# Weights converted in wider pieces, a smaller first group of chunks, and more seven-product pairs, in one kernel of retention and two MLPs

## The chip, the cores and the metric

The kernel runs on one core of one Trainium2 chip. The metric is the device time of one execution in microseconds, as the median of several runs. Inputs and weights lie in the chip's memory when it starts.

## The reference, cut to what matters

```python
# attention: B=4, H=8, S=576, D=64, with a decay mask in place of a softmax
scores = (q @ k.T) / sqrt(D)
ret = scores * where(i >= j, gamma[h] ** (i - j), 0.0)
x = (ret @ v)                       # laid out as 2304 tokens x 512
# first MLP, 512 -> 2048 -> 512
h = maximum(x @ moe_w_in, 0.0)
y = (h * h) @ moe_w_out
# second MLP, 512 -> 1536 -> 512
out = ((y @ moe2_w_a) * (y @ moe2_w_b)) @ moe2_w_out
```

The weights arrive as 64-bit floats, as pairs of 32-bit words. The rest is float32.

## The kernel before, in words

**Precision.** A float32 operand of a matmul is split into two parts of a shorter type (float32r): a high part, copied by ScalarE, and a low part, the difference, by VectorE. Each product of 128 x 128 weights with a block of tokens is three matmuls: high by high, low by high, high by low.

**Weights.** `w_float` (L347) turns 128 x 512 weights from 64-bit to 32-bit floats: a 512 KB load into a raw buffer (`wraw`, later `raw`), two ScalarE instructions that read the high words (L373) and the low words (L399), and four on VectorE: clamp (L377), shift and mask (L384), sign (L392), and the addition of the rounded low words (L403). The result lies in `wf` or `wl`.

**First group of chunks.** The hidden units come in chunks of 128: 16 in the first MLP, 12 in the second. The chunks in `FIRST` (0 to 5) of the first MLP are taken while attention runs. `load_first` (L528) converts and splits their up and down weights, which stay in the slots `w0` to `w11`. `mlps` walks five blocks of tokens (four of 512, one of 256): for each chunk `up` (12 matmuls), squares, and `down` (12 matmuls). The sums of a block leave through `evac_y` to memory (`y1`). Attention's steps are woven in: for each microsecond of MLP matmuls, `RATE` says how much of attention comes (L1380).

**The other chunks** (`CHUNKS[1]`: 6 to 15, `CHUNKS[2]`: 0 to 11) are run in `rest` (L939) in three passes of 768 tokens, first MLP then second. `x_prep` makes seven combinations of the pass's input, as of a 2 x 2 block matrix, each split (`xo`; the seventh in `xb`). A unit is a pair of chunks in the first MLP, one chunk (its a and its b weights) in the second. Its up-projection is done as seven products in place of eight (`group`, L1114), six matmuls of 384 columns each. The combinations of weights are made once by `keep_pair` (L479) and stored in memory (`kept`); for each unit `piece` (L1019) loads its four pieces (512, 512, 512, 256 columns) into `w` slots and splits them. The second MLP's first piece is stored split (`parts`, `PARTS`) in pass 0 and loaded whole in the later ones.

**Down-projections** of these chunks are either plain (`plain`, 24 matmuls a chunk) or, where `SEVENS` names a run of chunks, seven products over pairs (`sevens`, L1253, 42 matmuls a pair; combinations of the weights by `keep_outs`, L501). Their weights pass through five `w` slots (`out_piece`, L1087). Sums are added into `xt` by `put` (L1208).

**Order.** All steps are put into a `Plan`, each with its engines, a modelled cost and what it reads and writes. `Plan.order` (L108) fixes one order per engine by the latest time at which each step is due; all loads and stores go out from SyncE's queue in that order. `enter` (L898) gives back attention's buffers once nothing uses them, and takes the later ones (`xo`, `raw`, `wl`, `tmp`). Conversions of later weights are steps like any others; `AHEAD` pairs of them are put ahead of `enter`.

## Time and profile before

| | us |
|---|---|
| median of 3 runs | 853.67 (851.36 to 857.92) |
| the profiled execution | 855.08 |
| its span, first to last instruction | 853.4 |
| TensorE busy in it | 835.2 (98%) |
| VectorE busy | 732.1 (86%) |
| ScalarE busy | 581.4 (68%) |

In the profile PE is TensorE's matmuls, PEld its weight loads, DVE VectorE, ACT ScalarE, SP SyncE; L234 is line 234 of the kernel, which for matmuls, copies and differences is the line of a helper. Records of neighbouring instructions of one engine overlap a little: the start of the next comes before the recorded end of the last, so what one costs its engine is read from start to start.

### The profile page before, as it was taken

What the parts mean: (1) busy time and instruction counts of PE and PEld (TensorE: products, weight loads), DVE (VectorE), ACT (ScalarE), POOL (GpSimd) and SP (SyncE); (2) the same over time, 40 slices, a digit from 0 to 9 for tenths busy, and PEclk for the clock granted to TensorE, in tenths of its full rate; (3) what the DMA queues carried; (4) which work ended last, traced back from release to release, by engine and by line L of the source; (5) the groups of instructions that cost most, each with busy time, mean ns of one, the idle gap of its engine ahead of it and who ended that gap; (6) DMA issues with size and microseconds to landing.
All of it is one profiled execution on the core that took longest, in us unless ns stands there. A gap on an engine that the chain in (4) does not pass through costs nothing.

```text
span 853.4 us, 17622 instructions
## 1 busy us (share of the span) xinstructions
PE 835.2 (98%) x6540; PEld 802.4 (94%) x6540; DVE 732.1 (86%) x1444; ACT 581.4 (68%) x1209; POOL 0.7 (0%) x6
## 2 busy tenths in 40 slices
PE   6799999999999999999999999999999999999998
PEld 6688888889999999999999999999999999999997
DVE  6999773878799998999999979989786789878785
ACT  5787663767888877878796565676556576556560
POOL 0000000000000000000000000000000000000000
PEclk9999999999999999999999999999999999999999
DMA  8966861379877667757847898755564545655432
GB/s 321 330 205 201 287 221 45 113 248 295 284 239 243 205 208 238 249 188 241 294 154 234 276 287 296 227 163 170 172 180 142 152 149 173 189 173 161 139 88 81
DMA packets 89734, 176.15 MB, mean 206 GB/s; under 512 B 9904, under 2 KB 34864, under 8 KB 89648
## 3 DMA queue, kind: packets, MB, share of 16 engines
q1 hardware_dynamic: 89504, 175.02, 64.2%
q8 instruction: 51, 0.84, 0.4%
q14 instruction: 35, 0.29, 0.1%
q10 hardware_dynamic: 144, 0.01, 0.0%
HBM read 134.75 MB, written 40.24 MB: 205 GB/s over the span
## 4 chain that ended last, share of the span: by engine, by line
PE 90%; DMA 4%; DVE 3%; ACT 2%; issue 1%; ACTq 0%
PE bank L234 90%; DMA w<-kept 2%; DMA raw<-w 1%; DVE w L243 1%; DMA vt<-vtab 0%; DVE wf L392 0%; DVE sc L731 0%; ACT w L240 0%; DVE xt L246 0%; DVE xt L698 0%; ACT bank L240 0%; DVE wf L403 0%; DVE pt L713 0%; ACT wf L373 0%; ACT sa L738 0%
## 5 line engine op out<-in xcount | busy, mean ns | idle before, releaser
L234 PE MATMUL bank<-xo,w 128*128 128x384 f32 x1838 | 389.5, 335 | 1.5 <-ACT bank L240 1.4
L234 PEld LDWEIGHTS bank<-xo,w 128*128 128x128 f32 x1838 | 324.4, 188 | 3.3 <-ACT bank L240 2.8
L234 PE MATMUL bank<-xb,w 128*128 128x384 f32 (+2 forms) x1044 | 230.1, 348 | 0.8 <-ACT r L855 0.7
L240 ACT CAST w<-w 128x512 fp32r<-128x512 f32 (+1 forms) x316 | 156.6, 518 | 81.7 <-DMA w<-kept 73.5
L234 PEld LDWEIGHTS bank<-xb,w 128*128 128x128 f32 x1044 | 183.8, 188 | 13.2 <-ACT r L855 1.1
L243 DVE TENSOR_TENSOR w<-w 128x512 fp32r<-128x512 f32 (+1 forms) x316 | 171.6, 562 | 17.9 <-ACT w L240 16.4
L234 PE MATMUL bank<-gh,w 128*128 128x384 f32 (+2 forms) x750 | 170.2, 352 | 0.0
L234 PEld LDWEIGHTS bank<-gh,w 128*128 128x128 f32 x750 | 132.3, 188 | 11.5 <-DVE gh L243 0.3
L234 PE MATMUL bank<-w,w 128*128 128x384 f32 x546 | 124.2, 335 | 0.5 <-DVE w L243 0.5
L234 PEld LDWEIGHTS bank<-w,w 128*128 128x128 f32 x546 | 97.2, 188 | 1.2 <-DVE w L243 0.9
L246 DVE TENSOR_TENSOR xt<-bank,xt 128x384 f32<-128x384 f32 x128 | 70.0, 555 | 8.7 <-PE bank L234 7.7
L240 ACT COPY bank<-bank 128x384 f32<-128x384 f32 x122 | 57.2, 469 | 18.6 <-PE bank L234 16.6
L234 PE MATMUL bank<-ghl,w 128*128 128x384 f32 x186 | 41.0, 335 | 0.0
L243 DVE TENSOR_TENSOR xo<-xt,xo 128x768 fp32r<-128x768 f32 x36 | 33.7, 955 | 1.7 <-ACT xo L240 1.7
L399 ACT ACTIVATE we<-raw 128x512 int32<-128x512 uint32 x48 | 31.8, 666 | 2.1 <-DVE wf L403 1.6
L243 DVE TENSOR_TENSOR gh<-g,gh 128x512 fp32r<-128x512 f32 (+2 forms) x40 | 24.5, 616 | 10.0 <-ACT g L858 8.7
L234 PEld LDWEIGHTS bank<-ghl,w 128*128 128x128 f32 x186 | 33.0, 188 | 0.1
L240 ACT CAST xo<-xt 128x768 fp32r<-128x768 f32 x36 | 29.1, 830 | 5.5 <-issue 5.1
L403 DVE CUSTOM_DVE_ANT_0 wf<-wf,we 128x1024 uint16<-128x1024 uint16 x45 | 30.8, 686 | 1.4 <-ACT we L399 0.9
L234 PEld LDWEIGHTS bank<-qkr 64*64 64x64 f32 x576 | 20.4, 147 | 8.1 <-DVE wf L377 3.3
L738 ACT COPY sa<-sc 128x384 f32<-128x384 f32 x16 | 14.8, 924 | 16.9 <-DVE sc L731 16.9
L234 PE MATMUL bank<-qkr 64*64 64x64 f32 x576 | 23.0, 235 | 3.3 <-DVE wf L377 2.9
(244 smaller groups left out, 971.3 us busy)
## 6 DMA issues: line engine op xcount, KB each, us to landing
w<-kept SPq DMA_DIRECT2D x167, 256.0 KB, 3.5
raw<-w SPq DMA_DIRECT2D x48, 512.0 KB, 4.6
w<-kept SPq DMA_DIRECT2D x149, 128.0 KB, 3.0
kept<-wf SPq DMA_DIRECT2D x49, 256.0 KB, 4.0
w<-parts SPq DMA_DIRECT2D x24, 512.0 KB, 3.6
kept<-wl SPq DMA_DIRECT2D x36, 256.0 KB, 4.4
wraw<-w SPq DMA_DIRECT2D x16, 512.0 KB, 6.4
vr<-vk SPq DMA_DIRECT2D x16, 448.0 KB, 4.9
```

Source lines behind the costliest of these rows:

```text
L234: T.matmul(o, l, r, start=start, stop=stop, skip_group_check=True)
L240: return lambda e: A.copy(o(), i()) if e == "ACT" else eng[e].tensor_copy(o(), i())
L243: return lambda e: eng[e].tensor_sub(o(), a(), b())
L246: return lambda e: eng[e].tensor_add(o(), a(), b())
L399: lambda e: A.activation(like(rest), lo(), AF.Copy, scale=LO_ULPS), [kraw], [ke],
L403: lambda e: V._custom_dve(ADD32_U16LIMBS, out=w().bitcast(U16), in0=w().bitcast(U16), in1=rest.bitcast(U16)),
L738: {"ACT": 540}, lambda e: A.copy(sa.rearrange("p (c d) -> p c d", d=D), by[:, :LONG - 1]), [ksc], [ksa]
```

## The change

- `FIRST` has four chunks (0 to 3), `CHUNKS[1]` twelve (4 to 15, six pairs). `RATE` is 0.5 in place of 0.35.
- `convert` takes 1024 columns (two chunks' or two kinds' weights) at a time, from one 1 MB load; only chunk 0 is converted in two pieces of 512. Two slots of 2048 columns (`wp`), one buffer for the low words (`we`, 1024), raw buffers twice as wide and half as many.
- `keep_pair` stores its combinations as two pieces, of 1024 and 768 columns, and `piece` loads and splits two in place of four. `PARTS` is empty: nothing is stored split.
- `keep_outs` is a task of its own for both MLPs; it makes combinations only for chunks that some run of `SEVENS` names. Two 256-column pieces of seven products are loaded into one 512-column slot and split by one pair of instructions.
- `SEVENS` also has the pair 10, 11 in the second MLP's pass 2, and chunks 4 to 7 in the first MLP's passes 1 and 2.
- The tasks are in one list: the first `AHEAD` (6, that is three pairs, up and down) stand ahead of `enter`. The slots `w8` to `w15` come with the later buffers. One more split tile (`ghl1`) and three more tiles (`more`) are there for intermediate results.

```diff
 
 NW = 16
 LENT = 1536
-AHEAD = 2
-FIRST = range(0, 6)
-CHUNKS = {1: range(6, 16), 2: range(0, 12)}
+AHEAD = 6
+FIRST = range(0, 4)
+CHUNKS = {1: range(4, 16), 2: range(0, 12)}
 N2 = 384
 PASSES = NT // (2 * N2)
 PIECES, OUTS = 8, 5
 RUN, LAG = {1: 2, 2: 3}, {1: 1, 2: 2.5}
-SEVENS = {(2, 0): [range(6, 12)], (2, 1): [range(0, 6), range(6, 12)], (2, 2): [range(0, 6), range(6, 10)]}
+SEVENS = {(2, 0): [range(6, 12)], (2, 1): [range(0, 6), range(6, 12)], (2, 2): [range(0, 6), range(6, 12)], (1,1):[range(4,8)],(1,2):[range(4,8)]}
 AFTER = 0.0
 SPAN = 0.8
 MORE = (2, 0, 6)
-PARTS = (0,)
-
-RATE = [0.35, 0.35, 0.35, 0.35, 0]
-
-WF, WL, WE, RAWS = 4, 4, 2, 2
+PARTS = set()
+
+RATE = [0.5, 0.5, 0.5, 0.5, 0]
+
+WP, WE, RAWS = 2, 1, 2
 SLOTS = dict(
-    g=2, r=2, gh=2, qkr=3, vr=3, tv=2, pt=2, sa=2, wraw=4, ys=4,
+    g=2, r=2, gh=2, qkr=3, vr=3, tv=2, pt=2, sa=2, wraw=2, ys=4,
 )
 
...
 
-    ring(big, "wf", [P, 512], F32, WF)
-    ring(big, "we", [P, 512], I32, WE)
+    ring(big, "wp", [P, 2048], F32, WP)
+    ring(big, "we", [P, 1024], I32, WE)
...
-    wslot = [big.tile([P, 2, 512], F32R, name=f"w{i}") for i in range(NW)]
+    ws = [big.tile([P, 2, 1024], F32R, name=f"w{i}") for i in range(len(FIRST))]
+    wslot = [w[:, j].rearrange("p (h n) -> p h n", h=2) for w in ws for j in range(2)]
     xt = big.tile([P, KT, NT], F32, name="xt")
...
 
     ring(ap, "ys", [P, 512], F32, SLOTS["ys"])
-    ring(ap, "wraw", [P, 1024], U32, SLOTS["wraw"])
+    ring(ap, "wraw", [P, 2, 1024], U32, SLOTS["wraw"])
     vt = ap.tile([P, 3 * NP], F32, name="vt")
...
+    def convert(w, kw, src, n):
+
         rest, ke = slot("we")
...
+
+        plan.add(dmac(P * 8 * n), dma(plane, source), w=[kraw], extra=exr)
         plan.add(
-            dmac(P * 4096),
-            dma(raw, lambda: like(src.bitcast(U32))), w=[kraw], extra=exr,
+            {"ACT": act(n)}, lambda e: A.activation(like(w()), hi().bitcast(F32), AF.Abs), [kraw], kw
...
-        plan.add(
-            {"DVE": dve2(512)},
+            {"DVE": dve2(n)},
...
+    def split(to, of, n, r, h, l):
+
...
+        plan.add({"ACT": act(n)}, copy(lambda: to()[0], of), r, h)
         plan.add(
             {"DVE": dve(n), "POOL": pool(n)},
-            sub(lambda: to()[:, 1, :n], of, lambda: to()[:, 0, :n]),
-            [kof, kto + (0,)], [kto + (1,)], ex,
+            sub(lambda: to()[1], of, lambda: to()[0]), r + (h if r else []), l,
         )
...
+    def fetch(to, sources, n, h, l, name, ex=()):
+
+        if name in parts:
+            plan.add(
+                dmac(P * 8 * n), dma(lambda: to()[2].bitcast(F32), lambda: parts[name]), [("parts", name)], h + l, ex
+            )
+            return
+        for cols, of, r in sources:
+            plan.add(
+                dmac(P * 4 * (cols.stop - cols.start)),
+                dma(lambda cols=cols: to()[1].bitcast(F32)[:, cols], lambda of=of: of), [r], l, ex,
+            )
+        split(lambda: to(), lambda: to()[1].bitcast(F32), n, l, h, l)
+        if name[:2] in PARTS and pass_["now"] < PASSES - 1:
+            parts[name] = dram.tile([P, 2, n], F32, name="parts" + "_".join(map(str, name)))
+            plan.add(
+                dmac(P * 8 * n), dma(lambda: parts[name], lambda: to()[2].bitcast(F32)), h + l, [("parts", name)]
+            )
...
+    def keep_pair(ph, c, src):
+
+        w, kw = slot("wp")
+        a, b = [kw + (0,)], [kw + (1,)]
+        convert(lambda: w[:, 512:1536], a + b, src, 1024)
+        combine(w, add, 0, 4, 5, b, a)
+        combine(w, sub, 1, 0, 2, [], a)
+        combine(w, sub, 4, 2, 4, a, b)
+        combine(w, sub, 6, 3, 1, a, b)
+        keep((ph, c, 0), lambda: w[:, :1024], a, 1024)
+        keep((ph, c, 1), lambda: w[:, 1024:1792], b, 768)
+
+    def keep_outs(ph, c, src):
+
+        w, kw = slot("wp")
+        a, b = [kw + (0,)], [kw + (1,)]
+        convert(lambda: w[:, 512:1536], b, src, 1024)
+        if any(c in r for k, rs in SEVENS.items() if k[0] == ph for r in rs):
+            combine(w, add, 0, 3, 5, b, a)
+            combine(w, sub, 6, 2, 3, b, a)
+            combine(w, sub, 1, 0, 2, b, a)
+            combine(w, sub, 7, 4, 1, b, a)
+            keep((ph, c, 4), lambda: w, a + b, 2048)
+        else:
+            keep((ph, c, 4), lambda: w[:, 512:1536], b, 1024)
+
+    def outs_of(ph, c, e):
+
+        c0, wide = c - (c - CHUNKS[ph][0]) % 2, kept[ph, c - (c - CHUNKS[ph][0]) % 2, 4]
+        at = {4: 512 * (c - c0), 5: -512, 6: 1024}[e] + (512 if wide.shape[1] == 2048 else 0)
+        return wide, at, ("kept", (ph, c0, 4))
+
+    tasks = []
+    for c in CHUNKS[1][::2]:
+        tasks.append(lambda c=c: keep_pair(1, c, w1[c:c + 2, :, 0, :].rearrange("c p n -> p c n")))
+        tasks.append(lambda c=c: keep_outs(1, c, w1[c:c + 2, :, 1, :].rearrange("c p n -> p c n")))
+    for c in CHUNKS[2][::2]:
+        for d in (c, c + 1):
+            tasks.append(lambda d=d: keep_pair(2, d, w2[d, :, 0:2, :]))
+        tasks.append(lambda c=c: keep_outs(2, c, w2[c:c + 2, :, 2, :].rearrange("c p n -> p c n")))
+
+    def load_first():
+        for c in FIRST:
+            i = 2 * (c - FIRST[0])
+            wt[c, 0], wt[c, 1] = i, i + 1
+            w, kw = slot("wp")
+            for j, m in ((0, 1), (1, 1)) if c == FIRST[0] else ((0, 2),):
+                cs = slice(512 * j, 512 * (j + m))
+                convert(lambda w=w, cs=cs: w[:, cs], [kw + (j,)], w1[c, :, j:j + m, :], 512 * m)
+
+                def to(i=i, j=j, m=m):
+                    x = ws[i // 2][:, j:j + m]
+                    return x[:, :, :512], x[:, :, 512:]
+
+                split(
+                    to, lambda w=w, cs=cs, m=m: w[:, cs].rearrange("p (a n) -> p a n", a=m), 512 * m, [kw + (j,)],
+                    [("w", i + j + a, 0) for a in range(m)], [("w", i + j + a, 1) for a in range(m)],
                 )
...
-    def keep_pair(ph, c, src_a, src_b):
-
-        a, b = slice(0, 256), slice(256, 512)
-        wa, ka = w_float(src_a)
-        wb, kb = w_float(src_b)
-        keep((ph, c, 0), wa, ka, 512)
-        ss, ks, exs = float_slot()
-
...
-        op(sub, ss, a, wb, a, wa, a, [ka, kb], [ks])
-        op(sub, wa, b, wa, b, ss, a, [ks], [ka])
-        keep((ph, c, 1), wb, kb, 512)
-        keep((ph, c, 2), ss, ks, 512)
-        keep((ph, c, 3), lambda: wa()[:, b], ka, 256)
...
-    def load_first():
-        for i, (c, j) in enumerate((c, j) for c in FIRST for j in range(2)):
-            wt[c, j] = i
-            w, kw = w_float(w1[c, :, j, :])
-            split(lambda i=i: wslot[i], ("w", i), w, kw, 512)
         del rings["wraw"][0][SLOTS["wraw"]:]
-        for c in CHUNKS[1][:2 * AHEAD:2]:
-            keep_first(c)
+        for task in tasks[:AHEAD]:
+            task()
...
-            raws.extend(late.tile([P, 1024], U32, name=f"raw{i}") for i in range(RAWS))
-            floats.extend(late.tile([P, 512], F32, name=f"wl{i}") for i in range(WL))
+            raws.extend(late.tile([P, 2, 1024], U32, name=f"raw{i}") for i in range(RAWS))
+            ws.extend(late.tile([P, 2, 1024], F32R, name=f"w{i}") for i in range(len(FIRST), NW // 2))
+            wslot.extend(w[:, j].rearrange("p (h n) -> p h n", h=2) for w in ws[len(FIRST):] for j in range(2))
             tmp.extend(late.tile([P, 512], F32, name=f"tmp{i}") for i in range(4))
-            tmp.append(late.tile([P, 2, N2], F32R, name="ghl"))
+            tmp.extend(late.tile([P, 2, N2], F32R, name=f"ghl{i}") for i in range(2))
+            tmp.extend(late.tile([P, N2], F32, name=f"more{i}") for i in range(3))
...
         state_["entered"] = plan.add({}, swap, extra=deps)
         hbanks[0] = [4, 5, 6, 7]
-        for c in CHUNKS[1][2 * AHEAD::2]:
-            keep_first(c)
-        for c in CHUNKS[2][::2]:
-            for d in (c, c + 1):
-                keep_pair(2, d, w2[d, :, 0, :], w2[d, :, 1, :])
-            keep_outs(c)
+        for task in tasks[AHEAD:]:
+            task()
...
 
         def piece(u):
             pass_["now"] = units[u][1]
-            for q in range(4):
-                i = turn["piece"] % PIECES
+            ph, _, c = units[u]
+            for q, m in ((0, 1024), (1, 768)):
+                i = 2 * (turn["piece"] % (PIECES // 2))
                 turn["piece"] += 1
                 pieces[units[u], q] = i
                 plan.renew(("w", i))
-                fetch((units[u][0], units[u][2], q), i, 256 if q == 3 else 512)
+                plan.renew(("w", i + 1))
+
+                def to(i=i, m=m):
+                    w = ws[i // 2]
+                    return w[:, 0, :m], w[:, 1, :m], w[:, :, :m]
+
+                name = ph, q, c
+                whole = slice(0, m)
+                fetch(
+                    to, [(whole, kept[ph, c, q], ("kept", (ph, c, q)))], m,
+                    [("w", i, h) for h in range(2)], [("w", i + 1, h) for h in range(2)], name,
+                )
 
...
             pass_["now"] = p
             i = ofree.pop(0)
             plan.renew(("w", i))
-            uses[i] = 2 if todo[0][0] == "whole" else len(todo)
-            for t, what in enumerate(todo):
-                outs[what[1]] = i, t
-                if what[0] == "whole":
-                    fetch(what[2], i, 512)
-                else:
-                    fetch_half(what[2], what[3], i, t)
+            uses[i] = 2 if todo[0][5] == 512 else len(todo)
+            sources, n_ = [], 0
+            for key, ph, c, e, s, m in todo:
+                outs[key] = i, n_ // 256
+                wide, at_, k = outs_of(ph, c, e)
+                cs = slice(at_ + 256 * s, at_ + 256 * s + m)
+                sources.append((slice(n_, n_ + m), wide[:, cs], k))
+                n_ += m
+
+            def to(i=i, n_=n_):
+                x = wslot[i][:, :, :n_]
+                return x[:, 0], x[:, 1], x
+
+            fetch(to, sources, n_, [("w", i, 0)], [("w", i, 1)], (ph, 4 if len(todo) == 1 else 5, *(y for x in todo for y in x[2:5])), [state_["entered"]])
```

In `group`, `PRODUCTS` names the same seven products with their new places in the two pieces, and each waits for the whole piece that it reads.

## Rows read from the trace of the kernel before

**Rows 1.** The page's first part: busy time of each engine.
```profile
PE 835.2 (98%) x6540; PEld 802.4 (94%) x6540; DVE 732.1 (86%) x1444; ACT 581.4 (68%) x1209; POOL 0.7 (0%) x6
```
**Rows 2.** Windows by stage: length, busy us (instructions) by engine, granted clock, DMA share, GB/s.
```profile
0.00:211.50 211.50, 199.43 (x2884) 169.88 (x2885) 167.68 (x312) 142.68 (x267) 0.67 (x6) 0.99 0.69 226
211.50:449.00 237.50, 236.97 (x1367) 235.84 (x1367) 223.40 (x435) 198.15 (x404) 0.00 (x0) 1.00 0.71 231
449.00:545.00 96.00, 94.77 (x543) 93.81 (x543) 89.16 (x190) 58.37 (x123) 0.00 (x0) 1.00 0.84 273
545.00:853.40 308.40, 304.02 (x1751) 302.88 (x1749) 251.86 (x509) 182.19 (x416) 0.00 (x0) 1.00 0.51 154
```
**Rows 3.** Windows of 25 us, the first two and the sixth (PE, PEld, DVE, ACT, POOL).
```profile
0.00:25.00 25.00, 16.66 (x464) 15.80 (x466) 18.53 (x37) 14.35 (x27) 0.67 (x6) 1.00 0.90 318
25.00:50.00 25.00, 21.26 (x394) 18.16 (x392) 22.95 (x45) 21.23 (x39) 0.00 (x0) 0.93 0.86 292
...
125.00:150.00 25.00, 25.00 (x448) 20.62 (x448) 8.84 (x16) 8.60 (x19) 0.00 (x0) 1.00 0.21 71
```
**Rows 4.** The chain that ended last: start us, us, what; first and last load wait.
```profile
322.95 5.50 DMA w<-kept
...
619.51 3.84 DMA w<-kept
```
**Rows 5.** Timeline of TensorE, three stretches: start us, us, instruction, count.
```profile
182.49 2.20 PE L234 MATMUL bank<-xb,w 128*128 128x512 f32 x9
184.53 1.75 PE L234 MATMUL bank<-gh,w 128*128 128x512 f32 x7
...
210.12 1.60 PE L234 MATMUL bank<-gh,w 128*128 128x256 f32 x12
211.56 2.34 PE L234 MATMUL bank<-xo,w 128*128 128x384 f32 x11
...
640.14 1.72 PE L234 MATMUL bank<-xb,w 128*128 128x384 f32 x9
641.70 0.68 PE L234 MATMUL bank<-xo,w 128*128 128x384 f32 x3
```
**Rows 6.** Timeline of VectorE, 41 to 43 us.
```profile
41.41 0.68 DVE L243 TENSOR_TENSOR w<-wf,w 128x512 fp32r<-128x512 f32 x1
42.01 0.62 DVE L698 TENSOR_TENSOR xt<-bank,gt 128x448 f32<-128x448 f32 x1
```
**Rows 7.** Groups by line and shape: count, busy us, mean ns, idle before.
```profile
L243 DVE TENSOR_TENSOR w<-w 128x512 fp32r<-128x512 f32 x167 | 114.2, 688 | 13.6 <-ACT w L240 12.5
...
L243 DVE TENSOR_TENSOR w<-w 128x256 fp32r<-128x256 f32 x149 | 60.6, 421 | 4.3 <-ACT w L240 3.9
L243 DVE TENSOR_TENSOR xo<-xt,xo 128x768 fp32r<-128x768 f32 x36 | 33.7, 955 | 1.7 <-ACT xo L240 1.7
...
L240 ACT CAST xo<-xt 128x768 fp32r<-128x768 f32 x36 | 29.1, 830 | 5.5 <-issue 5.1
```
**Rows 8.** DMA issues: count, KB each, median us to landing.
```profile
raw<-w SPq DMA_DIRECT2D x48, 512.0 KB, 4.6
...
w<-parts SPq DMA_DIRECT2D x24, 512.0 KB, 3.6
...
xt<-y SPq DMA_DIRECT2D x3, 1536.0 KB, 6.8
```
**Rows 9.** Windows of 10 us, instructions on attention's `qkr` alone (PE, PEld).
```profile
150.00:160.00 10.00, 0.46 (x16) 0.32 (x12) 1.00 0.33 107
```
**Rows 10.** Windows of 10 us, instructions on `xo` alone (PE, PEld, DVE, ACT).
```profile
160.00:170.00 10.00, 0.00 (x0) 0.00 (x0) 2.78 (x3) 1.25 (x2) 1.00 0.37 120
```
**Rows 11.** Timeline of TensorE, 28 to 40 us: idle before in brackets.
```profile
32.08 0.48 PE L234 MATMUL bank<-qkr 64*64 64x64 f32 x4 [2.86 <-DVE wf L377]
...
38.94 3.01 PE L234 MATMUL bank<-xb,w 128*128 128x512 f32 x12 [0.69 <-ACT r L855]
```

More of the change, by code (lines that the diff above doesn't have):

```diff
@@ L106, in renew, with succeed @@
         self.before[key] = self.users.pop(key, ())
+    def succeed(self, new, old):
+        self.users[new] = list(self.users.get(old, ()))
     def order(self):
@@ L301, in tile_retention_two_mlps @@
     lent = slice(LENT, LENT + 512)
-    rings["wraw"][0] += [xt[:, k:k + 2, lent].bitcast(U32) for k in (0, 2)]
-    lenders = [("wraw", SLOTS["wraw"] + i) for i in range(2)]
+    rings["wraw"][0].append(xt[:, :, lent].bitcast(U32))
+    lenders = [("wraw", SLOTS["wraw"])]
     mask = ap.tile([P, C], F32, name="mask")
@@ L320, in tile_retention_two_mlps @@
     wt = {}
-    state_ = {"entered": None, "loads": 0, "floats": 0, "sums": 0}
+    state_ = {"entered": None, "loads": 0, "sums": 0}
     raws = []
@@ L523, in keep_first, with keep, combine @@
-    def keep_first(c):
-        keep_pair(1, c, w1[c, :, 0, :], w1[c + 1, :, 0, :])
+    def keep(name, of, r, n):
+        kept[name] = dram.tile([P, n], F32, name="kept" + "_".join(map(str, name)))
+        plan.add(dmac(P * 4 * n), dma(lambda: kept[name], of), r, [("kept", name)])
+    Q = [slice(256 * i, 256 * i + 256) for i in range(8)]
+    def combine(w, fn, o, x, y, r, k):
+        plan.add({"DVE": dve(256)}, fn(lambda: w[:, Q[o]], lambda: w[:, Q[x]], lambda: w[:, Q[y]]), r, k)
+    def keep_pair(ph, c, src):
[8 more added lines that the diff above has]
+        keep((ph, c, 1), lambda: w[:, 1024:1792], b, 768)
@@ L944, in rest @@
         gtiles = [(lambda i=i: rings["gh"][0][i][:, :, :n], ("gh", i)) for i in range(2)]
-        gtiles.append((lambda: tmp[4], ("ghl", 0)))
+        gtiles += [(lambda i=i: tmp[4 + i], ("ghl", i)) for i in range(2)]
         flat1 = xb[1].rearrange("p k n -> p (k n)")
@@ L954, in rest, with tile_ @@
         ttiles += [(lambda i=i: tmp[i][:, :n], ("tmp", i)) for i in range(4)]
-        more = [(lambda i=i: rings["wf"][0][i][:, :n], ("wf", i)) for i in range(WF)]
-        more += [(lambda i=i: floats[i][:, :n], ("wf", WF + i)) for i in range(WL)]
-        more += [(lambda i=i: rings["we"][0][i].bitcast(F32)[:, :n], ("we", i)) for i in range(WE)]
-        more += [
-            (lambda i=i, j=j: raws[i].bitcast(F32)[:, 512 * j:512 * j + n], ("late", i))
-            for i in range(RAWS) for j in range(2)
-        ]
+        ttiles += [(lambda i=i: tmp[6 + i], ("more", i)) for i in range(3)]
+        more = []
+        for tag, size, wide in (("wp", WP, 2048), ("we", WE, 1024), ("late", RAWS, 2048)):
+            for i in range(size):
+                for j in range(wide // n):
+                    def tile_(tag=tag, i=i, j=j):
+                        x = raws[i].rearrange("p a b -> p (a b)") if tag == "late" else rings[tag][0][i]
+                        return x.bitcast(F32)[:, n * j:n * j + n]
+                    more.append((tile_, (f"{tag}{j}", i), (tag, i)))
         turn = {"piece": 0}
@@ L1077, in rest @@
                 for c in dict.fromkeys(r[1] for r in what):
-                    wanted.append((p, [("whole", (ph, p, c), (ph, c, 4))]))
+                    wanted.append((p, [((ph, p, c), ph, c, 4, 0, 512)]))
             else:
@@ L1120, in f @@
                     for b in o[2:]:
-                        mm(b, wslot[pieces[unit, 0]][:, 0, :P], xo[0][:, 0, 0], True, True)
+                        mm(b, ws[pieces[unit, 0] // 2][:, 0, :P], xo[0][:, 0, 0], True, True)
                 w = pieces[unit, 0]
-                plan.add(mmc(n, n), f, [("w", w, 0)] + [k + (0,) for k in xkeys[0]], ko[2:])
+                plan.add(mmc(n, n), f, [("w", w, h) for h in range(2)] + [k + (0,) for k in xkeys[0]], ko[2:])
             for i, q, s, b, start in PRODUCTS:
                 w = pieces[unit, q]
-                rd = [("w", w, 0), ("w", w, 1)] + [k + (h,) for k in xkeys[i] for h in range(2)]
+                rd = [("w", w + v, h) for v in range(2) for h in range(2)] + [k + (h,) for k in xkeys[i] for h in range(2)]
                 for k in range(2):
@@ L1362, in rest @@
             if unit == MORE:
-                tfree.extend(more)
+                for x, k, old in more:
+                    plan.succeed(k, old)
+                    tfree.append((x, k))
             for k, _ in enumerate(group(unit, (4, 5, 6, 7), u == 0)):
```

146 lines of the change are left out of this document (34 added, 112 removed).

## The prediction, made before the change was run

> **What bounds the kernel now.** I read the shares of busy time first. TensorE is busy 98% of the span; VectorE follows with 86%, ScalarE with 68% [rows 1]. A matmul record overlaps its neighbours, so the busy share alone says little. The windows by stage settle it: attention with the first group of chunks ends at 211.5 us, the second group at 449, the first pass of the second MLP at 545; behind 211.5 us TensorE stands still for 237.50 − 236.97 = 0.5, 96.00 − 94.77 = 1.2 and 308.40 − 304.02 = 4.4 us, most of the last behind the final matmul. Ahead of it, it is idle 12.1 us, all within the first 50 us [rows 2, 3]. The chain that ended last says the same: matmuls, with only six waits on a load from 50 us on, the first at 322.95 and the last at 619.51 us [rows 4]; the chain walks back through the whole transfer, while TensorE, which had other work for most of it, lost under a microsecond at each. So the time is the sum of the matmuls, plus a start of which 12.1 us is idle, plus a few microseconds of stalls.
>
> VectorE is the second limit: 89.16 of 96 us and 223.40 of 237.5 [rows 2]. What is not due yet (the conversion of later weights) fills its gaps, so a full VectorE is no stall by itself, but there is little room.
>
> **TensorE's sum.** From start to start, nine 512-wide matmuls take 184.53 − 182.49 = 2.04 us, 0.2267 each; nine 384-wide ones 641.70 − 640.14 = 1.56, 0.1733 each; twelve 256-wide ones 211.56 − 210.12 = 1.44, 0.12 each [rows 5].
> - Chunks 4 and 5 leave the first group: per chunk and block 24 matmuls (4 x 3 up, 4 x 3 down), four blocks 512 wide and one 256: 2 x 24 x (4 x 0.2267 + 0.12) = 49.3 us off.
> - They become a sixth pair of the second group: per pass 42 matmuls up (seven products of six) and 48 down, three passes: 270 x 0.1733 = 46.8 us on.
> - Five more pairs go down as seven products: 42 matmuls for 48 each: 30 x 0.1733 = 5.2 us off (two pairs in each of passes 1 and 2 of the first MLP, one in pass 2 of the second).
>
> Together 7.7 us off.
>
> **VectorE's sum.** Its cost is from start to start too: 0.60 us for 512 (41.41 to 42.01), under a record of 0.68 [rows 6]; the mean records of 256, 512 and 768 (421, 688, 955 ns) lie on a line of 1.043 ns an element [rows 7], of which the last 0.08 overlap the next. I take 1.042n + 67 ns: 0.335 (256), 0.468 (384), 0.60 (512), 0.87 (768) and, as an estimate from that line, 1.135 (1024).
> - Conversion: 68 of four instructions become 35, 33 of them twice as wide; 33 x 4 x 0.068 saved = −9.0. Sums and differences of quarters: twelve more of 256, +4.0.
> - First group: its splits −2.6, the halves of eight 512 and two 256 activations −5.5.
> - Three more units in the first MLP: six operations of 384 each, +8.4. Its pieces: 15 x 2.135 become 18 x 2.0, +4.0; its down-projection weights: 30 of 512 become 28 + 14, +7.2; adds into xt: 72 become 92, +9.4.
> - Seven products need 7 more operations of 384 a pair (11 for 4 lowers): five pairs, +16.4.
> - Second MLP: first quarter no longer kept split (24 more splits), less narrow pieces: −2.0 in pass 0, +9.6 later; eight adds fewer, −3.7.
>
> In all about +36, of which about +27 falls ahead of the end of the second MLP's first pass. ScalarE: −8.9 (33 x 2 fixed parts of 0.135), +9.1 (splits), −14.9 and −2 (first group), +18.5 (units), +9 (sevens): +11, which leaves it near 70%, no bound. DMA: some 2.5 MB less in 358 weight transfers for 522; the loads grow to 1 MB, which lies between the 4.6 us of 512 KB and the 6.8 us of 1.5 MB [rows 8]. I take 6 us, between the two; 4.6 and 9.2 (twice 4.6) are the ends. It is hidden while two raw buffers run ahead.
>
> [...]
>
> **Does VectorE hold?** To 545 us it was busy 167.68 + 223.40 + 89.16 = 480.2 us, idle 64.8 (11.9%) [rows 2]. After: 507 of 545 − 2.5 − 24 x 0.1733 = 538.3 us; 31.3 us, 5.8%, may stay idle. In the second group it was idle just 14.1 of 237.5, 5.9% [rows 2]. What it can win back: at 125 to 150 us it did 8.84 us of work [rows 3], because the two pairs prepared ahead were done and the buffers for later weights come only when attention's are given back; six tasks (three pairs) ahead fill that. So it can just hold. In the first group's stage the same work stands beside 49 us less of TensorE: attention now gets half of what the MLP's matmuls take instead of 0.35. From 35 us to its last rows at 150 to 160 [rows 9] that was some 31 us of attention in 89 of MLP (120/1.35); the same 31 now stand in 62 of MLP, so attention ends near 128 us, and its buffers turn into the second group's. The preparation of x, done from 150 to 170 us for a first use at 211.5 [rows 5, 10], had 40 us of room; 20 us of it after 128, for a first use near 163, leave 15.
>
> **Waits that change.** (a) Chunk 1's up weights now come with its down weights in one piece: ScalarE and VectorE each take one 1024 before anything of it is usable, and VectorE is a queue in order; the second chunk's up step stands at 38.94 us, with a 0.69 us wait already [rows 11]. From −1 us (five of eight conversions are done by then anyway, and fewer loads follow) to +5: I take 0. (b) The first pieces of the second group lie on chunks 0 and 1's slots, given back after the last block's steps. Behind chunk 0 come five half chunks of 12 x 0.12 = 7.2 us; load, copy and subtraction of 1024 columns take about 3.6 + 1.0 + 1.1 [rows 7, 8] and their signals (ScalarE's 1.0 is an estimate from its 830 ns for 768). Before, more chunks lay between. From 0 to +3 with a busy DMA: I take +1. (c) Two conversion slots, one buffer for the low words, so the next piece's low words wait for the last's addition: ScalarE has others to do; what is queued behind it is conversion, and behind that a fetch one unit ahead. From −1.5 (the load waits of [rows 4] go with fewer transfers) to +4: I take 0.
>
> Profiled execution: 855.08, 853.4 of span and 1.7 around it; −7.7 + 1 gives 848.4. It lay 1.4 above the median 853.67, so the forecast for a median is **847.0**.
>
> **Rivals.**
> *The start gets lighter.* Eight halves of chunks are loaded and converted rather than twelve, while DMA is 90% and 86% busy in the first 50 us and TensorE loses 12.1 us there, plus a stretch at a granted clock of 0.93 in mean [rows 3]. If a third of the idle goes: 853.7 − 7.7 − 4 = 842. Against it: up to 32 us the chain is attention's, not the weights'.
> *Wide pieces come late.* Waits (a) and (b) at +3 and +2, and a clock loss of 25 x 0.07 = 1.7 again: the 2.86 us stop ahead of 32.08 us was followed by that stretch [rows 3, 11]. 846 + 6 = 852.
> *VectorE becomes the bound* up to the second MLP's first pass, and the time goes up. It decides from an idle share over 5.8%. If the share falls only halfway, from 11.9% to 9%, 507/0.91 = 557 us stand where TensorE needs 538: +19, so 846 + 19 = 865. For it: the extra adds of the seven products come where VectorE had 5.9% left. Against: it was 94% busy there and cost TensorE 0.5 us.
> *Nothing comes of it:* that nothing of the 7.7 comes would need the removed matmuls not to be on the path; with TensorE 98% busy I give that no chance of its own.
>
> **How the numbers follow.** Forecast 0.50 (own range 843.5 to 850.5), lighter start 0.25, late pieces 0.15, VectorE 0.10. A measurement here tells about 1% from no change: 845.1 and 862.2 are the borders. Faster: 0.25 and a fifth of 0.50: 0.35. Slower: 0.10. Same: 0.55. The range 839.5 to 860 holds the first three and the start of the last.
>
> **What would show it.** 48 fewer wide matmuls in equal terms: 192 fewer of 512, 48 fewer of 256, 240 more of 384. The border between the groups near 162 us, the second MLP from about 442. VectorE near 768 us busy, its 125-to-150 hole gone. TensorE idle in the first 50 us near 12, after that near 7, its tail counted. I am wrong if TensorE's windows show over 10 us idle between 160 and 545 with waits on VectorE (the last rival), or if the first 50 us lose less than 8 or more than 16.

## The result, and the profile after

| | before | after |
|---|---|---|
| median, us | 854.74 (6 runs, 851.36 to 857.92) | 846.76 (6 runs, 846.39 to 848.09) |
| ratio | | 0.991, 95% interval 0.9883 to 0.9937 |
| the profiled execution, us | 855.08 | 846.60 |
| its span, us | 853.4 | 844.9 |

The change takes 8.0 us off, 0.9%. The interval does not reach 1, so the gain is real, but it lies just inside the 1% that I had called "same". The forecast was 847.0 for the median and 848.4 for the profiled execution.

First the page's line of busy time, which answers to [rows 1]:

```profile
PE 826.7 (98%) x6540; PEld 801.8 (95%) x6540; DVE 761.8 (90%) x1269; ACT 595.7 (71%) x1067; POOL 0.7 (0%) x6
```

TensorE's share stays at 98% and its time falls. VectorE goes from 86% to 90%: it took on 29.7 us of work in a shorter span. The windows by stage, to be laid beside [rows 2] (length, busy time by engine as there, granted clock, DMA share). The border between the groups lies at 162 us (211.5 before), the second MLP begins at 442 (449) and its second pass at about 541 (545; counted in matmuls, 541 lies a little later in the work, for its row has 573 where the row before has 543):

```profile
0.00:50.00 50.00, 37.43 (x867) 33.04 (x868) 40.89 (x66) 32.53 (x53) 0.67 (x6) 0.97 0.83 293
50.00:162.00 112.00, 111.26 (x1766) 92.70 (x1765) 99.81 (x160) 79.44 (x138) 0.00 (x0) 1.00 0.75 254
162.00:442.00 280.00, 278.58 (x1611) 277.46 (x1611) 267.60 (x444) 234.44 (x429) 0.00 (x0) 1.00 0.67 228
442.00:541.00 99.00, 99.00 (x573) 99.00 (x572) 96.21 (x163) 61.19 (x99) 0.00 (x0) 1.00 0.74 247
541.00:844.90 303.90, 300.48 (x1731) 299.60 (x1729) 257.28 (x440) 188.11 (x352) 0.00 (x0) 1.00 0.44 135
```

The fourth row decides about VectorE: it is busy 96.21 of 99 us, and TensorE does not stand still for one of them. Up to 541 us VectorE worked 40.89 + 99.81 + 267.60 + 96.21 = 504.5 us (507 forecast). The 25-us windows beside [rows 3]:

```profile
0.00:25.00 25.00, 15.25 (x428) 14.55 (x428) 18.84 (x36) 13.18 (x24) 0.67 (x6) 1.00 0.90 311
25.00:50.00 25.00, 22.18 (x439) 18.49 (x440) 22.04 (x31) 19.36 (x30) 0.00 (x0) 0.93 0.76 275
...
125.00:150.00 25.00, 25.00 (x150) 20.85 (x146) 24.39 (x38) 17.74 (x31) 0.00 (x0) 1.00 0.57 192
```

TensorE is idle 9.75 + 2.82 = 12.6 us at the start (12.1 before). VectorE's hole from 125 to 150 us is filled: 24.39 us of work where 8.84 stood. The chain that ended last, from the border on (start, us, what; beside [rows 4]):

```profile
158.43 4.10 DMA w<-kept
...
167.90 8.04 DMA y<-tmp
...
179.58 650.13 PE bank L238 x3749
...
829.74 11.78 PE bank L238 x65
841.52 0.02 issue
841.54 0.56 DVE xt L250
```

From 179.58 us on, the chain is one unbroken row of 3749 matmuls: the six waits on loads of [rows 4], from 322.95 to 619.51 us, are gone. The last two rows show an end that I had not counted: the last pair of chunks now goes down as seven products, and behind its final matmul stands one addition. Before, it was this one row of the same view:

```profile
847.91 2.12 DVE xt L246 x4
```

The border itself, on TensorE's timeline (in brackets the idle time before and what ended it):

```profile
162.20 1.60 PE L238 MATMUL bank<-gh,w 128*128 128x256 f32 x12
163.71 0.84 PE L238 MATMUL bank<-xo,w 128*128 128x384 f32 x3
164.92 1.66 PE L238 MATMUL bank<-xo,w 128*128 128x384 f32 x8 [0.37 <-DVE w L247]
...
171.26 2.36 PE L238 MATMUL bank<-xo,w 128*128 128x384 f32 x12 [0.65 <-ACT bank L244]
...
179.58 0.44 PE L238 MATMUL bank<-ghl,w 128*128 128x384 f32 x1 [0.40 <-DVE ghl L247]
```

The first use of `xo` stands at 163.71 us (211.56 before, [rows 5]): 47.85 us earlier, of 49.3 worked out. Three stops of 1.4 us in all lie there, the first for a split of weights, as step (b) had it. The groups of VectorE's wide instructions (count, busy us, mean ns, idle before) and the loads (count, KB, median us to landing):

```profile
L250 DVE TENSOR_TENSOR xt<-bank,xt 128x384 f32<-128x384 f32 x140 | 75.9, 553 | 5.8 <-PE bank L238 4.2
...
L247 DVE TENSOR_TENSOR w<-w 128x1024 fp32r<-128x1024 f32 x54 | 65.9, 1220 | 1.2 <-ACT w L244 1.0
...
L399 DVE CUSTOM_DVE_ANT_0 wp<-wp,we 128x2048 uint16<-128x2048 uint16 x33 | 40.2, 1219 | 0.2
```

```profile
raw<-w SPq DMA_DIRECT2D x24, 1024.0 KB, 6.0
```

The 1024-wide difference has a record of 1220 ns: on the line drawn through the three narrower widths (154 + 1.043 x 1024 = 1222). The 1 MB load lands in 6.0 us, the value taken between the two ends.

### The profile page after: what moved, and what is told of

Read it like the earlier page. It is cut to its first block, busy times and chain, and to the rows that moved or that the text cites. A ratio compares the mean times of both kernels' runs of the same rounds, so it can differ in the third digit from the quotient of the medians.

```text
span 844.9 us, 16923 instructions
## 1 busy us (share of the span) xinstructions
PE 826.7 (98%) x6540; PEld 801.8 (95%) x6540; DVE 761.8 (90%) x1269; ACT 595.7 (71%) x1067; POOL 0.7 (0%) x6
## 4 chain that ended last, share of the span: by engine, by line
PE 95%; DMA 2%; DVE 2%; issue 1%; ACT 0%; DVEq 0%; ACTq 0%
PE bank L238 95%; DMA y<-tmp 1%; DMA w<-kept 0%; DMA vt<-vtab 0%; DVE sc L700 0%; ACT w L244 0%; DVE xt L667 0%; DVE pt L682 0%; DVE wp L399 0%; DVE wp L388 0%; DVE xb L247 0%; DVE wp L380 0%; DVE wp L373 0%; ACT ghl L1182 0%; DVE w L247 0%
## 5 line engine op out<-in xcount | busy, mean ns | idle before, releaser
L247 DVE TENSOR_TENSOR w<-w 128x512 fp32r<-128x512 f32 (+3 forms) x211 | 185.1, 885 | 14.1 <-ACT w L244 13.8
L244 ACT CAST w<-w 128x512 fp32r<-128x512 f32 (+3 forms) x211 | 161.4, 781 | 51.6 <-DMA w<-kept 50.3
L238 PE MATMUL bank<-gh,w 128*128 128x384 f32 (+2 forms) x606 | 138.4, 350 | 0.0
L238 PE MATMUL bank<-ghl,w 128*128 128x384 f32 x372 | 84.1, 335 | 0.4 <-DVE ghl L247 0.4
L238 PEld LDWEIGHTS bank<-ghl,w 128*128 128x128 f32 x372 | 66.2, 188 | 1.1 <-DVE ghl L247 0.7
L399 DVE CUSTOM_DVE_ANT_0 wp<-wp,we 128x2048 uint16<-128x2048 uint16 (+1 forms) x35 | 41.6, 1189 | 0.2
L247 DVE TENSOR_TENSOR wp<-wp 128x256 f32<-128x256 f32 (+1 forms) x82 | 34.2, 426 | 0.2
L395 ACT ACTIVATE we<-raw 128x1024 int32<-128x1024 uint32 x24 | 27.6, 1150 | 5.5 <-DVE wp L399 5.2
L388 DVE SCALAR_TENSOR_TENSOR wp<-raw,wp 128x1024 uint32<-128x1024 uint32 x24 | 29.2, 1219 | 0.0
L369 ACT ACTIVATE wp<-raw 128x1024 f32<-128x1024 f32 x24 | 27.4, 1141 | 1.9 <-DMA kept<-wp 1.9
```

Source lines behind the costliest of these rows:

```text
L238: T.matmul(o, l, r, start=start, stop=stop, skip_group_check=True)
L244: return lambda e: A.copy(o(), i()) if e == "ACT" else eng[e].tensor_copy(o(), i())
L247: return lambda e: eng[e].tensor_sub(o(), a(), b())
L369: {"ACT": act(n)}, lambda e: A.activation(like(w()), hi().bitcast(F32), AF.Abs), [kraw], kw
L388: lambda e: V.scalar_tensor_tensor(out=like(wu()), in0=hi(), scalar=0xC0000000, in1=like(wu()), op0=ALU.bitwise_and, op1=ALU.bitwise_or),
L395: lambda e: A.activation(like(rest[:, :n]), lo(), AF.Copy, scale=LO_ULPS), [kraw], [ke],
```

## The experiments

Each of the twelve kernels is the kernel after with one to three edits. Two quantities, both chosen after the runs were seen, tell them apart: TensorE's idle time from 475 to 600 us, in and just behind the second MLP's first pass, where its weights are needed for the first time; and how many 512-column halves of weights have had their last conversion instruction by 440 us, about where the second MLP begins (68 are to be done in all; 66 come in wide pieces, two to an instruction). The table gathers both, from each kernel's profiled execution; the text below takes the runs by question. The kernel before ran beside each group of runs with a median of its own, from 854.7 to 856.5 us, so small differences are read from the ratio to before rather than from the times.

| kernel | us, median | ratio to before | halves by 440 us | TensorE idle 475 to 600 us | VectorE busy, us |
|---|---|---|---|---|---|
| five pairs plain | 853.3 | 0.998 | 60 | 0.0 | 740.4 |
| six chunks first | 846.8 | 0.990 | 54 | 0.0 | 745.7 |
| no clamp | 849.4 | 0.992 | 54 | 0.3 | 738.5 |
| narrow, no clamp | 847.9 | 0.992 | 54 | 0.0 | 747.9 |
| **after** | 846.8 | 0.991 | 52 | 0.0 | 761.8 |
| other order of tiles | 847.5 | 0.989 | 52 | 0.0 | 761.2 |
| narrow | 858.0 | 1.003 | 48 | 6.5 | 766.3 |
| clamp three times | 880.1 | 1.028 | 46 | 20.4 | 796.8 |
| six chunks first, four more pairs | 855.8 | 1.000 | 46 | 8.7 | 763.8 |
| the same, pieces stored split | 866.1 | 1.013 | 46 | 15.9 | 747.2 |
| four more pairs, no clamp | 864.8 | 1.009 | 44 | 10.9 | 759.3 |
| four more pairs | 865.9 | 1.012 | 42 | 14.7 | 781.9 |
| four more pairs, pieces stored split | 877.6 | 1.026 | 40 | 22.4 | 763.3 |

The runs fall in two: with 52 halves or more, TensorE loses 0.3 us there at most; with 48 or fewer, it loses 6.5 us or more. VectorE's total does not sort them: 761.8 holds, 747.2 and 759.3 don't. Two cautions go with all of these runs. `Plan.order` lays out every engine's instructions anew for each edit, so none of them changes VectorE's work alone. And the first 50 us differ from trace to trace in a way that the edits don't explain: TensorE is idle there for 11.4 to 13.8 us, at a mean granted clock of 0.90 to 1.00.

### Which part carries the time

**Five pairs plain again.** `SEVENS` goes back to what it was before.

```diff
-SEVENS = {(2, 0): [range(6, 12)], (2, 1): [range(0, 6), range(6, 12)], (2, 2): [range(0, 6), range(6, 12)], (1,1):[range(4,8)],(1,2):[range(4,8)]}
+SEVENS = {(2, 0): [range(6, 12)], (2, 1): [range(0, 6), range(6, 12)], (2, 2): [range(0, 6), range(6, 10)]}
```

> The changed kernel (median 846.8 us), with the five added pairs of chunks taken down plainly again. If the time is the sum of TensorE's matmuls: 30 more of 384 columns, 30 x 0.1733 = +5.2 us, and the end with four additions in place of one, +0.5 us: 852.5 us. If VectorE sets the end: 16 us less on it, so part of the 5.2 comes back, 849 us or less. If the wide pieces bring the gain by themselves: 847 us.

Measured: 853.3 us (850.91 to 860.47, 12 runs), ratio to before 0.9983 (0.9964 to 1.0003). The five pairs are worth 6.5 us: the 5.2 of their matmuls, the 0.5 at the end, and a rest that the spread of these runs does not settle (in the profiled execution the first 50 us ran at a granted clock of 0.90, those of after at 0.97). Without them nothing measurable is left of the gain.

**Six chunks in the first group.** `FIRST`, `CHUNKS` and `RATE` as before, the pieces wide, the five pairs kept (those of the first MLP on chunks 6 to 9).

```diff
-FIRST = range(0, 4)
-CHUNKS = {1: range(4, 16), 2: range(0, 12)}
+FIRST = range(0, 6)
+CHUNKS = {1: range(6, 16), 2: range(0, 12)}
...
-RATE = [0.5, 0.5, 0.5, 0.5, 0]
+RATE = [0.35, 0.35, 0.35, 0.35, 0]
```

> The changed kernel with six chunks in the first group and five pairs in the second again (RATE 0.35, the two early seven-product runs now on chunks 6 to 9); wide pieces and all seven-product pairs kept. If the sum of matmuls decides: 49.3 - 46.8 = +2.5 us, 849.3 us; 848 if the 1.5 us stall at the border between the groups goes at once. If a lighter start matters: twelve halves of chunks to convert rather than eight, TensorE idle over 14 us in the first 50 us and 851 us or more.

Measured: 846.78 us (845.29 to 847.97, 5 runs), ratio 0.9901 (0.9882 to 0.992), the same as after, where 849.3 was expected. By the sum TensorE has 2.5 us more to do, but its first 212 us run better. The windows of this kernel:

```profile
0.00:50.00 50.00, 38.35 (x818) 33.94 (x822) 41.64 (x67) 34.32 (x54) 0.67 (x6) 0.93 0.88 317
...
50.00:212.00 162.00, 162.00 (x2082) 136.68 (x2073) 129.42 (x199) 109.23 (x184) 0.00 (x0) 1.00 0.67 227
```

Idle 11.65 us at the start and none from 50 to 212; after loses 12.57, 0.74 and 1.42 up to 442 us. That is 3.1 us less, of which 0.67 comes back between 450 and 475. Of these, the 0.9 at the start lies within what kernels with the same first group differ by; the 2.2 behind it are attention's and the border's stops. So the smaller first group seems to have won 2.5 us of matmuls and paid most of them for such stops. The part of the change with the largest terms of the sum (−49.3 + 46.8) is worth nothing that can be measured here; the two intervals together leave room for some 3 us either way.

**Narrow instructions.** The pieces, loads and buffers stay wide, but each of the six conversion instructions is issued for 512 columns at a time (the clamp stands for all six):

```diff
-            {"DVE": dve2(n)},
+        for h in range(m):
...
+                {"DVE": dve2(512)},
...
-                out=w(), in0=w(), scalar1=F64_MIN, scalar2=F64_MAX, op0=ALU.max, op1=ALU.min
+                    out=plane_(w(), h), in0=plane_(w(), h), scalar1=F64_MIN, scalar2=F64_MAX, op0=ALU.max, op1=ALU.min
```

> The changed kernel with each of the six conversion instructions issued twice, for 512 columns each; loads, buffers and order of tasks as they are. VectorE gets 33 x 4 x 0.068 = 9.0 us more, ScalarE 33 x 2 x 0.135 = 8.9. If the matmuls decide and VectorE holds: VectorE near 771 us busy, time within 1.5 us of 846.8. If the gain hangs on the wide instructions, or VectorE sets the end: 852 to 856 us.

Measured: 857.98 us (855.13 to 860.23, 12 runs), ratio 1.003 (1.0014 to 1.0047), 11.2 us over after and 2 over the upper of the two answers that I had expected. First the stretch from 475 to 600 us, in after and in this kernel:

```profile
475.00:600.00 125.00, 125.00 (x723) 125.00 (x722) 120.38 (x200) 82.68 (x141) 0.00 (x0) 1.00 0.64 209
```

```profile
475.00:600.00 125.00, 118.48 (x660) 115.25 (x660) 122.79 (x231) 83.31 (x150) 0.00 (x0) 0.99 0.65 224
```

TensorE's timeline in it:

```profile
530.48 3.28 PE L238 MATMUL bank<-xo,w 128*128 128x384 f32 x18
537.70 1.32 PE L238 MATMUL bank<-xb,w 128*128 128x384 f32 x6 [3.93 <-DVE more L250]
538.86 3.95 PE L238 MATMUL bank<-xo,w 128*128 128x384 f32 x12
542.65 1.23 PE L238 MATMUL bank<-ghl,w 128*128 128x384 f32 x6
```

And the chain at that place:

```profile
499.96 29.14 PE bank L238 x168
529.59 0.68 DVE wp L407
530.61 0.60 DVE wp L407
531.55 0.60 DVE wp L423
...
537.97 1.13 DVE w L247
```

The chain leaves TensorE at 529 us for VectorE's conversion instructions (L407 and L423 are this kernel's sign and addition) and the split of weights. TensorE stands for 3.93 us at 534. The wait is put down to a sum of seven products (`more`), but that sum only stood in VectorE's queue behind conversion that had become due. Then twelve matmuls take 542.65 − 538.86 = 3.79 us, 0.316 each in place of 0.1733 and 1.7 us more in all: the granted clock from 525 to 550 us was 0.93 in mean, and 0.07 of these 25 us is 1.75.

### Is it VectorE, and which of its hours?

**The clamp three times**, which changes no value and adds two instructions a piece on VectorE:

```diff
+        plan.add(
+            {"DVE": dve2(n)},
+            lambda e: V.tensor_scalar(
+                out=w(), in0=w(), scalar1=F64_MIN, scalar2=F64_MAX, op0=ALU.max, op1=ALU.min
+            ),
+            w=kw,
+        )
...
```

> The changed kernel with the clamp of each conversion done three times (same values). VectorE gets 2 x (33 x 0.60 + 2 x 0.34) = 41 us more, all of it ahead of about 541 us, where it was idle 36.5 us in all. If VectorE becomes the bound there once its idle share is used up, as the last rival of the prediction has it: 860 to 870 us, with TensorE idle some 15 to 20 us between 160 and 560 us waiting for VectorE. If VectorE is no limit at all: 847 us.

Measured: 880.13 us (876.38 to 881.43, 4 runs), ratio 1.0279 (1.025 to 1.0308): 33 us over after, and 10 over the range expected. The same place gives way:

```profile
475.00:600.00 125.00, 104.64 (x547) 101.88 (x546) 116.94 (x193) 72.03 (x114) 0.00 (x0) 0.90 0.67 232
```

20.4 us of idle there, and a granted clock of 0.90 in mean over 125 us.

**No clamp**, wide and narrow: 35 (or 68) instructions fewer on VectorE.

```diff
-        plan.add(
-            {"DVE": dve2(n)},
-            lambda e: V.tensor_scalar(
-                out=w(), in0=w(), scalar1=F64_MIN, scalar2=F64_MAX, op0=ALU.max, op1=ALU.min
-            ),
-            w=kw,
-        )
```

> The changed kernel with the clamp left out, nothing else. VectorE 20.5 us less. If VectorE just holds there, as the forecast said, nothing is to be won: 846.8 us within 1. If it already cost time: 842 or less.

> The run with narrow conversion instructions (858.0 us) with the clamp left out. VectorE 66 x 0.34 = 22 us less than there and some 14 less than in the changed kernel; ScalarE keeps its 8.9 us more and each piece its longer chain. If VectorE's sum made the narrow form late: back to 847 us. If ScalarE or the chain did: 855 us or more.

Measured: wide 849.44 us (846.72 to 851.91, 6 runs; ratio 0.9916, 0.9892 to 0.9939), narrow 847.87 (846.61 to 852.49, 6 runs; 0.9916, 0.9889 to 0.9942). With VectorE relieved, narrow instructions cost nothing:

```profile
475.00:600.00 125.00, 125.00 (x723) 125.00 (x722) 116.69 (x205) 82.22 (x149) 0.00 (x0) 1.00 0.59 193
```

So what made the narrow kernel late is VectorE's time, not ScalarE's extra instructions or the longer row of steps from a load to a stored piece, for these are in this kernel too (short of what the new order by itself does). And the wide kernel gains nothing without its clamp: in after, VectorE's time does not yet count. Its median lies 2.7 us over after's, but the kernel before was slower beside it too (856.5 us against 854.7), and the ratios, 0.9916 and 0.991, are the same.

**Four more pairs.** Chunks 8 to 11 of the first MLP go as seven products too, in passes 1 and 2; with four chunks first and with six (there chunks 10 to 13).

```diff
-SEVENS = {(2, 0): [range(6, 12)], (2, 1): [range(0, 6), range(6, 12)], (2, 2): [range(0, 6), range(6, 12)], (1,1):[range(4,8)],(1,2):[range(4,8)]}
+SEVENS = {(2, 0): [range(6, 12)], (2, 1): [range(0, 6), range(6, 12)], (2, 2): [range(0, 6), range(6, 12)], (1,1):[range(4,8),range(8,12)],(1,2):[range(4,8),range(8,12)]}
```

> The changed kernel with four more pairs as seven products (chunks 8 to 11 in passes 1 and 2 of the first MLP). TensorE: 4 x 6 x 0.1733 = 4.2 us less. VectorE: 4 x 7 x 0.468 = 13 us more, in the stretch where it is 96% busy. If TensorE's sum alone decides: 842.6 us. If VectorE has no more room there (narrow instructions with 9 us more cost 11 us): the 4.2 are lost again and more, 848 to 856 us, TensorE idle in the second MLP's first pass (500 to 580 us).

> Six chunks in the first group (as in the run before with 846.8 us) and four more pairs as seven products, 10 to 13. TensorE's sum alone: 842.6 us. VectorE is idle 51 us up to 545 us there in place of 36, but 33 of them stand in the first group's stretch. If work moves freely along VectorE: 842.6 to 844; if the room must be where the pairs are (10 us idle from 212 to 545): 846 to 854.

Measured: 865.9 us (861.57 to 868.11, 6 runs; ratio 1.012, 1.0095 to 1.0146) and 855.78 (854.34 to 857.47, 12 runs; 1.0001, 0.9988 to 1.0014). TensorE has 24 matmuls, 4.2 us, less to do than in after and in the kernel with six chunks first, and the time is 19 and 9 us longer: both beyond the worst that I had expected (856 and 854). The profiled execution of the first was the fastest of its six, 861.6 us, so its trace shows less than the usual loss.

**The same without the clamp**, which takes 22.6 us off VectorE:

> The run with four more pairs on the changed kernel (865.9 us), and the clamp of every conversion left out: the smallest and largest weights are not brought into range. VectorE 33 x 0.60 + 2 x 0.34 = 20.5 us less, no transfer more; against the changed kernel 13 - 20.5 = -7 us. If VectorE's sum is what made the four pairs late: the conversions are done in time, TensorE is not idle between 200 and 800 us, and its 4.2 us come in: 842.6 us. If tiles, ScalarE's copies or the load queue hold the pairs: 860 us or more as before.

Measured: 864.8 us (859.82 to 866.92, 6 runs), ratio 1.0088 (1.0056 to 1.012). That refuted the theory as I had put it: VectorE's total, 759.3 us, lay under after's, and 18 us were still lost (15 by the ratios). By what was written ahead of the run, this is the answer for "tiles, ScalarE's copies or the load queue"; none of these was tested by itself. The stretch ahead of the loss tells part of it. This is VectorE's addition, the last instruction of a conversion, from 240 to 440 us, in three kernels: five pairs plain (no pair of the first MLP as seven products), after (four), and four more pairs (eight).

```profile
L399 DVE CUSTOM_DVE_ANT_0 wp<-wp,we 128x2048 uint16<-128x2048 uint16 x12 | 14.6, 1218 | 0.0
```

```profile
L399 DVE CUSTOM_DVE_ANT_0 wp<-wp,we 128x2048 uint16<-128x2048 uint16 x8 | 9.7, 1218 | 0.0
```

```profile
L399 DVE CUSTOM_DVE_ANT_0 wp<-wp,we 128x2048 uint16<-128x2048 uint16 x3 | 3.7, 1221 | 0.0
```

Twelve pieces, eight, three. Up to 240 us all thirteen kernels have done 32 to 38 halves, these three 36 each; their difference arises in this stretch. (With narrow instructions or three clamps half or more of the shortfall against after, 2 of 4 and 4 of 6 halves, is there by 240 us already.) Adding up VectorE's groups in the stretch (records, which overlap a little): conversion and combinations of weights 65.8, 45.5, 21.2 us, all the rest 145.8, 174.7, 205.0. So with each four pairs the rest grows by 29 to 30 us of records in these 200 us, and conversion, which is due later, gets what is left of an engine that is full. Not all of it is the pairs' own: over the whole kernel four more pairs add 20.1 us of busy time (781.9 − 761.8), so some work that stood elsewhere was moved into the stretch. Taking the clamp away relieves the whole kernel, but this stretch only by the clamps that fall into it. Here are after's stretch, and two windows of the run without clamp:

```profile
240.00:440.00 200.00, 200.00 (x1155) 199.99 (x1155) 195.86 (x331) 168.54 (x313) 0.00 (x0) 1.00 0.61 207
```

```profile
120.00:240.00 120.00, 118.21 (x798) 111.50 (x798) 100.51 (x159) 95.50 (x168) 0.00 (x0) 0.99 0.74 255
240.00:440.00 200.00, 199.96 (x1154) 199.64 (x1153) 197.51 (x341) 174.71 (x338) 0.00 (x0) 1.00 0.55 178
```

In the run without clamp VectorE has 19.5 us idle of the first 120 and 2.5 of the next 200. Five pieces are done in the second, two more than with the clamp: the relief became idle time ahead of the stretch that needed it. Why no more is converted ahead of 240 us, with VectorE idle, no run told apart: loads, buffers or the fixed order may hold it. What TensorE then waits for, from 500 us on, is not VectorE's time alone either. The chain of this run passes three times through a store of converted weights:

```profile
496.28 7.57 DMA kept<-wp
...
508.58 8.70 DMA kept<-wp
...
526.95 4.83 DMA kept<-wp
```

Behind each comes a conversion's step on ScalarE, at 504.98, 517.31 and 531.88 us: there are only two `wp` slots, and a slot is free when its store has landed (the second store at 517.28 us, the step behind it 0.03 us later). From 480 to 560 us ScalarE waits 5.1 us for such stores and 9.8 for the one buffer of low words (`we`), and VectorE has 3.1 us idle from 500 to 525 us, where TensorE loses 1.9. No run with more slots or buffers was made.

**Pieces stored split.** To take the splits of later passes off VectorE, the first MLP's pieces are stored split in pass 0 and loaded so in passes 1 and 2, with four more pairs; four chunks first and six.

```diff
-PARTS = set()
+PARTS = {(1, 0), (1, 1)}
```

> The run with four more pairs on the changed kernel, and with it the first MLP's pieces stored split in its pass 0 and loaded whole in passes 1 and 2: VectorE 12 x (1.135 + 0.87) = 24 us less, ScalarE 12 x 1.7 = 20 less, 11 MB more written and as much more read. If VectorE's room is what the pairs lack: 842.6 us, with TensorE not idle between 200 and 800 us. If it is their waits (tiles, copies on ScalarE, banks): as without the stored pieces.

> Six chunks in the first group, four more pairs, pieces of the first MLP stored split (five pairs: VectorE 10 x 2.0 = 20 us less). If VectorE's room decides: 842.6 us, or 841 if the border and the start stay as quiet as with six chunks. If the added transfers cost: 845 or more.

Measured: 877.57 us (876.93 to 878.1, 4 runs; ratio 1.0258, 1.0237 to 1.028) and 866.12 (865.3 to 868.34, 4 runs; 1.0129, 1.0106 to 1.0152): worse by 12 and 10 us than the runs that they were to mend. A window of the first, and its load queue's longest waits from 200 to 440 us (in total, times, longest):

```profile
240.00:440.00 200.00, 198.78 (x1145) 198.00 (x1143) 182.81 (x324) 160.06 (x316) 0.00 (x0) 1.00 0.76 262
```

```profile
SPq L256 <- PE bank L238: 115.9, 53, 7.9
SPq L256 <- DVE wp L247: 23.8, 5, 10.8
SPq L256 <- DMA parts<-w: 15.5, 4, 8.4
SPq L256 <- DMA kept<-wp: 10.5, 4, 4.6
```

VectorE now has 17 us idle in the stretch, and still only four pieces are converted in it. The DMA share is 0.76 (0.51 with four more pairs alone), and the one queue of loads stands 15.5 us for stores of these parts, a wait that only the two kernels with such stores have (15.6 in the other), and 10.5 for stores of combinations (4.2 with four more pairs alone). Its long waits for matmuls and for VectorE are in after too (119.5 and 26.6). So weights seem to wait for transfers here. Whether the queue's order or the DMA engines' load makes them late is not shown.

**Another order of tiles.** In the list from which intermediate results take their tiles, `more` comes ahead of `tmp`.

```diff
-        ttiles += [(lambda i=i: tmp[i][:, :n], ("tmp", i)) for i in range(4)]
         ttiles += [(lambda i=i: tmp[6 + i], ("more", i)) for i in range(3)]
+        ttiles += [(lambda i=i: tmp[i][:, :n], ("tmp", i)) for i in range(4)]
```

> The changed kernel with the three new tiles handed out ahead of the four whose sums are still being stored at the border between the groups. The store of 8.0 us in the chain at 168 us goes, and with it 0.4 us of idle TensorE: 846.4 us; no change within the noise if the load behind it is as late; worse by up to 5 if the order of tiles matters elsewhere.

Measured: 847.49 us (845.16 to 847.96, 6 runs), ratio 0.9893 (0.9873 to 0.9912): no difference. The store is gone from the chain at the border, and from 162 to 442 us TensorE is idle for 0.8 us in place of 1.4, which the spread of the runs hides. No kernel tried beats after by more than these measurements tell.

## Why the prediction was right, point by point

- **What bounds the kernel.** Right: TensorE's matmuls; the chain is theirs from 179.58 us to the end.
- **TensorE's sum, −7.7.** The span fell by 8.5. Up to the first use of `xo`, 47.85 us went for 49.3: 1.45 short, of which the first 50 us lost 0.5 and attention's last stretch to 162 us 0.7. From there to the last matmul 39.9 came for 41.6: 1.7 better, with 1.4 of stops at the border added and 2.2 of stops in the middle gone, and some 0.9 that I can't assign. The end gave 0.6. Of the sum's terms, the experiments bear out the five pairs (6.5 us measured, 5.7 with the end expected); the 2.5 us of the smaller group did not show in the time.
- **VectorE's sum, +36.** It measured +29.7 busy, but busy time counts the end of a record only where no next one overlaps it. Counted as the forecast counted, all records less 85 ns for each, VectorE's work grows from 706 to 742 us, +35. Its additions into `xt` came as counted (a group of 128 became 140, +20 − 8). The merged instructions saved about what the starts had said: narrow against wide without the clamp is 747.9 − 738.5 = 9.4 us for 99 instructions, with the clamp 766.3 − 761.8 = 4.5 for 132. But six copies out of banks more went to VectorE in the one and six fewer in the other, worth some 3 us each, which leaves about 6 and 8; at 0.067 us each these are 6.6 and 8.8.
- **Does VectorE hold?** Right, and by less than I knew. The step that 507 us fit into 538.3 held: 504.5 in 541, idle 6.7%. Its measure was poor. I set a border at an idle share up to the second MLP's first pass; in these thirteen kernels what goes with the loss is how much conversion is done by 440 us, and with more pairs that falls short from 240 to 440 us. The narrow instructions (9 us more of VectorE by the sum, 4.5 by busy time) are enough to pass the border, at 11 us.
- **Wait (a), 0.** Right: none of the stops in the first 50 us is for weights; they are attention's (2.12 us for `sa`) and for the first tokens' split (1.81 and 0.45, `xb`).
- **Wait (b), +1.** 1.4 us in three stops, one of them for a split of weights.
- **Wait (c), 0.** It came out as −2.2, a little beyond its lower end (−1.5): the load waits of [rows 4] all went. What the step feared, two conversion slots that hold up the next piece, shows beside it, in the run with four more pairs and no clamp.
- **The rivals.** A lighter start did not come: idle 12.6 for 12.1, and six chunks in wide pieces start no worse. Late wide pieces did not come. VectorE as the bound did not come in this kernel, but its mechanism shows right beside it: with narrow instructions, or with four more pairs. (That the latter came to 866, where the rival's price was 865, is luck: the price was worked out for another amount of work. The price of late wide pieces, 846 + 6, is 6.7 by its own terms, which changes nothing.)
- **The number.** That the median hit within 0.3 us is partly luck. For the profiled execution 848.4 was forecast and 846.60 came: the change is 8.5 us where 6.7 was summed, 2.2 of it from the waits in the middle. The forecast for the median then took off 1.4 us, because the profiled execution before lay that far above the median of three; over six runs it lies 0.3 above, and after's lies 0.2 below its own.

What the prediction did not have: the end shorter by 0.6 us, and that by parts the gain lies in the five pairs, with the wide instructions as what makes room for them on VectorE.

## What to carry to other kernels

Where one engine is 98% busy, count its instructions by their start-to-start time, and the time follows (here 7.7 us summed, 8.5 measured on the span); an edit that only moves work can return a small gain in stops (here 2.5 us of matmuls against 2.2 of stops), so sum it separately. Where a second engine is nearly full, don't ask for its busy share but for its deadlines: what must be done by which stage, and which stretch ahead of that stage is full. Work added there displaced the work due next (with four more pairs, three wide pieces converted from 240 to 440 us in place of eight), and the bill came a stage later (14.7 us of idle TensorE from 475 to 600 us), under another instruction's name; relief elsewhere did little here (864.8 us without the clamp, 865.9 with it).
